# Query rows in overlapping groups of four, one buffer for a batch's rows, loads held back, in a fused attention and gated convolution

## The chip, the cores and the metric

The kernel runs on one core of one Trainium2 chip. The metric is the device time of one execution in microseconds (us); of several executions the median is taken. The core has five engines that run their own instruction streams: TensorE (PE), VectorE (DVE), the scalar engine (ACT), GpSimd (POOL) and SyncE (SP). SP issues the DMAs of this kernel's main part; they move data between HBM and SBUF, or inside SBUF.

## The reference

Agent attention, B = 4, N = 12800, C = 128, 49 agents, followed by a gated block with a causal convolution of five taps along the sequence:

```python
def sm(a, b):
    s = scale * (a @ b.transpose(0, 2, 1))
    s = s - s.max(-1, keepdims=True)
    e = np.exp(s)
    return e / (e.sum(-1, keepdims=True) + 1e-09)
a2k = sm(agents, k)
agent_v = a2k @ v
q2a = sm(q, agents)
x = q2a @ agent_v
...
for k in range(K):
    gate_pre += conv_w[k][None, None, :] * xp[:, k:k + S, :]
gate = 1.0 / (1.0 + np.exp(-gate_pre))
val = x @ w_val
return (gate * val @ w_out).astype(np.float32)
```

## The kernel before

A batch's 12800 positions are cut into 10 units of 1280, two units make a segment (20 in all), and 25 chunks of 512 positions a batch (the last one of all is halved) are what TensorE works on behind the softmax.

**Per batch.** Key scores are made (L376), their maximum is taken, they are exponentiated, and the agents' values are summed up (L480). Then the batch's weights are folded: since x is q2a times 49 rows, the value weights and the five convolution taps are multiplied with these 49 rows beforehand (gw at L541, wst), so that the chunks work on the rows of q2a and x is never formed. Weights and rows are float16, each split into a high part (hi) and the rest (lo), and hi x hi, hi x lo and lo x hi are summed.

**Per unit (queries, transposes).** Scores (L376), transposed on VectorE (sT), less their maximum (L750 on POOL, written to a ring `qw`), exp on ACT, sum, reciprocal and product on VectorE (L772). The float16 rows `pt` have 128 columns per block of 128 positions: lo in 0:49 (L794 on POOL, `w - hi`), hi in 49:98 (cast L779 on ACT), and 30 columns that repeat two of three hi columns (L784 on POOL). A transpose turns `pt` into 128 rows of 1280 positions: on TensorE for the first four units (L849), by a DMA transpose for the other 36 (L835). The rows go into one of four buffers `x1_` (ring NX = 4), one per segment, with 16 columns ahead of each. Of these the last four (HALO) hold the end of the segment before: POOL copies them (L819), or clears them at a batch's start (L816), when the transposes of the segment before have landed.

**x2.** What 128 rows have no room for, hi x lo for some hi rows, goes through a second tile `x2`: 19 hi rows, each five times, shifted by 0 to 4 positions, are copied from `x1_` by two DMAs inside SBUF (L884): 15 rows that stand three partitions apart (75 rows of x2) and four adjacent ones (20 rows). 95 of 128 partitions are in use.

**Per chunk.** The gate is five matmuls on x1, one per tap (L922), and one on x2 with 95 rows (L926); tanh on ACT (L935). The value is one matmul on x1 (L949) and one on x2 (L953). h is made on VectorE (L962), hh is its float16 part (ACT, L968), hl the rest (POOL, L973), and three matmuls with the output weights follow (L992, L993, L994). ACT scales the result (L1006), and a DMA on SP stores it (L1021).

**What sets the order.** TensorE's order is one long string written by hand (`order`). For the other engines, `Plan.order` places each step (with a cost written beside it) by list scheduling in a simulated time, and the program is then issued in the order of the steps' start times. SP's queue, in order, takes the loads (L369, 11 buffers `ld`), the transposes (L835), the x2 copies (L884) and the stores. A load is a step as soon as its buffer is free: the planner places it as early as the queue allows. `Plan.order` ends with

```python
self.start = start
return sorted(range(n), key=lambda i: (start[i], i))
```

Of the kernel before, what the change touches and what calls it, by code (L numbers as in the profile page):

```python
# [32 lines left out]
THREES = 15  # L33
NDUP = 2 * THREES
X2R = 19
X2CUTS = ((0, THREES, 3, 0.5), (THREES, X2R, 1, 0.3))

# [4 lines left out]
NX = 4  # L42
# [18 lines left out]
LAND = 1.4  # L61

# [5 lines left out]
class Plan:  # L68
# [25 lines left out]
    def order(self):  # L94
# [22 lines left out]
        at = [0.0] * n  # L117
# [56 lines left out]


@with_exitstack
def tile_agent_attention_gated_conv(
# [39 lines left out]
    qw = ring(NPT, [P, NBLK, A], F32, "qw")  # L217
# [3 lines left out]
    x1s = ring(NX, [P, PAD + SEG], F16, "x1_")  # L221
# [39 lines left out]
    tiny = const.tile([P, NBLK], F32, name="tiny")  # L261
    nc.scalar.dma_start(out=ag_sb, in_=agT)
# [6 lines left out]
    nc.vector.memset(x1s[0][:, 0:PAD], 0.0)  # L269
    for t in wst_sb:  # L270
        nc.gpsimd.memset(t[:, TAPS + 1 :, :], 0.0)
# [82 lines left out]
    def load(kind, b, u):  # L354
# [12 lines left out]
        for d, f, keys in parts:  # L367
            add(
                "dma", 0.4, lambda d=d, f=f: nc.sync.dma_start(out=d, in_=f), (), keys,  # L369
                1.57 / len(parts),  # L370
            )
# [132 lines left out]
    avT = const.tile([P, A], F32, name="avT")  # L504
    mx = const.tile([P, 2], F32, name="mx")
    gw = const.tile([P, TAPS, A], F32, name="gw")
    gs = const.tile([P, TAPS, A], F32, name="gs")
# [5 lines left out]
    def fold_weights(b):  # L513
# [19 lines left out]
        def normalise():  # L533
            dve.tensor_scalar_add(den, pt[:, 0:A], 1e-9)
            dve.reciprocal(out=den, in_=den)
            dve.tensor_tensor(out=avT, in0=pt[:, AP_ : AP_ + A], in1=den, op=ALU.mult)
# [5 lines left out]
                out=gw, in0=avT.unsqueeze(1).to_broadcast([P, TAPS, A]),  # L542
                in1=conv_sb.unsqueeze(2).to_broadcast([P, TAPS, A]), op=ALU.mult,
# [4 lines left out]
        def gate_scale():  # L548
# [16 lines left out]
                out=pv[:, 0:A], lhsT=wval_sb, rhs=avT, start=True, stop=True  # L565
# [4 lines left out]
        x2g = wst[:, TAPS + 1, 0 : TAPS * X2R].rearrange("p (r k) -> p k r", k=TAPS)  # L570
        x2v = wst[:, TAPS + 2, 0 : TAPS * X2R].rearrange("p (r k) -> p k r", k=TAPS)
        ghi = wst[:, 0:TAPS, 0:A]
        vhi = wst[:, TAPS, 0:A]

        def threes(x):

            if len(x.shape) == 2:
                return x[:, 0 : 3 * THREES].rearrange("p (i r) -> p i r", r=3)
            return x[:, :, 0 : 3 * THREES].rearrange("p k (i r) -> p k i r", r=3)

        def rest(out, full, s, hi):
            dve.scalar_tensor_tensor(
                out=out, in0=full, scalar=rs[:, s : s + 1], in1=hi,
                op0=ALU.mult, op1=ALU.subtract,
            )

        def val_weights():
# [9 lines left out]
            dve.tensor_scalar_mul(vhi, pv[:, 0:A], rs[:, 1:2])  # L597
            pv3, hi3 = threes(pv[:, 0:A]), threes(vhi)
            rest(
                wst[:, TAPS, 2 * A :].rearrange("p (i r) -> p i r", r=2),  # L600
                pv3[:, :, 0:2], 1, hi3[:, :, 0:2],
            )
            rest(x2v[:, HALO, 0:THREES], pv3[:, :, 2], 1, hi3[:, :, 2])
            rest(x2v[:, HALO, THREES:], pv[:, 3 * THREES : A], 1, vhi[:, 3 * THREES :])

        def gate_weights():
            dve.tensor_scalar_mul(ghi, gw, rs[:, 0:1])
# [6 lines left out]
        def gate_rest_pool():  # L614
            def less(out, full, hi):
                nc.gpsimd.tensor_tensor(out=out, in0=full, in1=hi, op=ALU.subtract)

            gs3, hi3 = threes(gs), threes(ghi)
            twos = wst[:, 0:TAPS, 2 * A :].rearrange("p k (i r) -> p k i r", r=2)
            for r in range(2):  # L620
                less(twos[:, :, :, r], gs3[:, :, :, r], hi3[:, :, :, r])
            less(x2g[:, :, 0:THREES], gs3[:, :, :, 2], hi3[:, :, :, 2])
            less(x2g[:, :, THREES:], gs[:, :, 3 * THREES :], ghi[:, :, 3 * THREES :])

        def gate_rest():
            gw3, hi3 = threes(gw), threes(ghi)
            twos = wst[:, 0:TAPS, 2 * A :].rearrange("p k (i r) -> p k i r", r=2)
            for r in range(2):
                rest(twos[:, :, :, r], gw3[:, :, :, r], 0, hi3[:, :, :, r])
            rest(x2g[:, :, 0:THREES], gw3[:, :, :, 2], 0, hi3[:, :, :, 2])  # L630
            rest(x2g[:, :, THREES:], gw[:, :, 3 * THREES :], 0, ghi[:, :, 3 * THREES :])
# [3 lines left out]
        if b == 0:  # L635
            add("pool", 0.4, gate_scaled, ["gw", "rsg"], ["gs"])
            add("act", 0.4, lambda: nc.scalar.copy(out=ghi, in_=gs), ["gs"], [(*w_, "g")])
            add("pool", 1.0, gate_rest_pool, ["gs", (*w_, "g")], [(*w_, "r")])
        else:
# [4 lines left out]
            lambda: nc.scalar.copy(out=wst[:, 0:TAPS, A : 2 * A], in_=ghi),  # L644
# [3 lines left out]
            "act", 0.22, lambda: nc.scalar.copy(out=wst[:, TAPS, A : 2 * A], in_=vhi),  # L648
# [84 lines left out]
    def queries(b, u):  # L733
# [4 lines left out]
        sT, d, e, w, r, sm = sts[x], qw[g % NPT], qw[g % NPT], qw[g % NPT], qr[x], qsm[x]  # L738
# [23 lines left out]
        def sums():  # L762
# [14 lines left out]
        p_ = ("pt", g % NPT)  # L777
        add(
            "act", 0.58, lambda: nc.scalar.copy(out=pt[:, :, A : 2 * A], in_=w),  # L779
# [3 lines left out]
            "pool", 0.44,  # L783
            lambda: nc.gpsimd.tensor_scalar(  # L784
                out=pt[:, :, 2 * A :].rearrange("p n (i r) -> p n i r", r=2),
                in0=w[:, :, 0 : 3 * THREES].rearrange("p n (i r) -> p n i r", r=3)[:, :, :, 0:2],
                scalar1=1.0, scalar2=0.0,
                op0=ALU.mult, op1=ALU.add,
# [3 lines left out]
        add(  # L792
            "pool", 1.09,
            lambda: nc.gpsimd.tensor_tensor(  # L794
                out=pt[:, :, 0:A], in0=w, in1=pt[:, :, A : 2 * A], op=ALU.subtract
            ),
            [("qw", g % NPT), (*p_, 0)], [(*p_, 1)],
        )
# [3 lines left out]

    def unit_rows(g):
        o = PAD + g % 2 * UNIT
        return x1s[g // 2 % NX][:, o : o + UNIT]

    def row_keys(s, halves):


        i = s % NX  # L810
        return [(x, i, h) for h in halves for x in ("x1", "x1b")] + [("x1h", i)] * (0 in halves)

    def halo(s):
        to = x1s[s % NX][:, PAD - HALO : PAD]
        if s * 2 % NU == 0:
            fn = lambda: nc.gpsimd.memset(to, 0.0)  # L816
            read = []
        else:
            fn = lambda: nc.gpsimd.tensor_copy(  # L819
                out=to, in_=x1s[(s - 1) % NX][:, PAD + SEG - HALO : PAD + SEG]  # L820
            )
            read = [(x, (s - 1) % NX, 1) for x in ("x1", "x1b")]

        read.append(("x2", (s - 1) % 3, UNIT, 0))
        add("pool", 0.1, fn, read, [("x1h", s % NX)])
# [40 lines left out]
    def shifts(b, u):  # L866
# [7 lines left out]
        x2, x1 = x2s[s % 3], x1s[s % NX]  # L874
        o = (g + 1 - n) % 2 * UNIT
        src = row_keys(s, range(0, g % 2 + 1))
        c = PAD - HALO + o
        for r0, r1, every, us in X2CUTS:
            first = A + (2 if every == 3 else 3 * THREES)
            rows = x1[first : first + 1 + (r1 - r0 - 1) * every : every, c : c + 1]  # L880
# [4 lines left out]
                    out=x2[r0 * TAPS : r1 * TAPS, o : o + n * UNIT],  # L885
# [255 lines left out]
    for i in plan.order():  # L1141
        plan.steps[i][2]()
# [44 lines left out]
```

## Time and profile before

Three executions took 425.65, 425.89 and 426.75 us, the median is 425.89.

| | value |
|---|---|
| median of the runs | 425.89 us |
| span of the profiled execution | 423.6 us |
| instructions in it | 10042 |
| DMA traffic | 127.62 MB, mean 301 GB/s |
| HBM read, written | 79.25 MB, 26.21 MB |

The profile is one execution, taken by the hardware profiler. Its span begins and ends with the first and last recorded work; what lies around it makes the 2.3 us to the median. Busy time is given per engine, and in rows of groups as `line engine operation out<-in, shape, count | busy us, mean ns of one | idle time just before, and what ended it`. In rows of waits the three numbers are us in total, times, and the longest. `PEclk` is the clock granted to TensorE in tenths. In rows of a timeline the start and the duration in us come first, and a bracket holds the idle time ahead and its releaser.

### The profile page before, as it was taken

To read this page: it belongs to the slowest core of one execution; us is meant where nothing else is said; L and a number is where in the kernel's file an instruction comes from. 1 tells how busy PE (TensorE), PEld (TensorE's weight loads), DVE (VectorE), ACT (ScalarE), POOL (GpSimd) and SP (SyncE) were. 2 spreads that over 40 slices of the span, in tenths; PEclk is the share of its full clock that TensorE was granted. 3 is DMA by queue.
4 is the path that set the end of the run, shared out by engine and by line. 5 is a ranking of instruction groups with operands and counts; after the bars stand their busy time and mean duration, and the time that the engine had idled before them with its cause. 6 is when DMAs were issued, how large, how long until landed. Compare 5 with 4: busy or idle time off the path is not lost.

```text
span 423.6 us, 10042 instructions
## 1 busy us (share of the span) xinstructions
PE 403.9 (95%) x3907; PEld 197.0 (47%) x3907; DVE 293.3 (69%) x562; ACT 301.5 (71%) x521; POOL 228.2 (54%) x263
## 2 busy tenths in 40 slices
PE   4979999999999999999999899999999989999995
PEld 1358434346555443446555343335555534344443
DVE  3757899867875978667795575767765678676231
ACT  1564568779966777678876486778876567788776
POOL 1002557654657565554566355574366277877553
PEclk9969999999999999999999899999999999999998
DMA  8999999999999999999999999999999977755733
GB/s 320 420 417 411 370 367 353 301 295 310 412 293 283 346 317 362 304 278 356 351 379 324 271 299 370 314 332 302 296 393 322 239 196 161 199 163 176 205 121 124
DMA packets 75129, 127.62 MB, mean 301 GB/s; under 512 B 50466, under 2 KB 50850, under 8 KB 75084
## 3 DMA queue, kind: packets, MB, share of 16 engines
q1 hardware_dynamic: 74940, 126.87, 96.9%
q8 instruction: 30, 0.49, 0.5%
q10 hardware_dynamic: 144, 0.13, 0.2%
q14 instruction: 15, 0.12, 0.1%
HBM read 79.25 MB, written 26.21 MB: 249 GB/s over the span
## 4 chain that ended last, share of the span: by engine, by line
PE 78%; DMA 9%; DVE 8%; ACT 1%; POOL 1%; issue 1%; SPq 0%; POOLq 0%; DVEq 0%; ACTq 0%
PE gate L922 23%; PE sc L376 17%; PE av L480 10%; PE val L949 5%; PE out L992 5%; PE val L953 5%; PE gate L926 5%; PE out L993 4%; DMA ld<-kT 4%; PE out L994 4%; DMA x<-pt 3%; DMA x<-x 2%; DVE h L962 1%; DVE qw L772 1%; DVE qsm L763 1%
## 5 line engine op out<-in xcount | busy, mean ns | idle before, releaser
L973 POOL TENSOR_TENSOR hl<-h,hh 128x512 f16<-128x512 f32 (+1 forms) x101 | 116.9, 1158 | 96.1 <-ACT hh L968 96.0
L922 PE MATMUL gate<-x,stat 128*128 128x512 f16 (+1 forms) x500 | 125.2, 380 | 0.2 <-ACT th L935 0.2
L962 DVE SCALAR_TENSOR_TENSOR h<-th,val 128x512 f32<-128x512 f32 x100 | 67.8, 678 | 66.8 <-PE out L993 26.2
L376 PE MATMUL sc<-ld,ag_sb 128*32 128x320 f32 x1280 | 101.5, 447 | 7.6 <-DMA ld<-kT 7.0
L935 ACT ACTIVATE th<-gate,unscale 128x512 f32<-128x512 f32 x100 | 68.3, 683 | 33.3 <-PE gate L926 31.7
L1006 ACT ACTIVATE ob<-out,oscale 128x512 f32<-128x512 f32 x98 | 67.3, 687 | 21.3 <-PE out L994 20.1
L922 PEld LDWEIGHTS <-stat 128*128 128x128 f16 x505 | 46.3, 97 | 63.7 <-issue 14.8
L968 ACT CAST hh<-h 128x512 f16<-128x512 f32 (+1 forms) x101 | 61.5, 609 | 17.2 <-DVE h L962 16.4
L750 POOL TENSOR_TENSOR qw<-sT,qmx 128x490 f32<-128x490 f32 x40 | 41.4, 1035 | 47.6 <-DVE qmx L745 47.5
L376 PEld LDWEIGHTS sc<-ld,ag_sb 128*32 128x32 f32 x1280 | 36.7, 111 | 59.4 <-issue 25.7
L480 PE MATMUL av<-ld,eT 128*32 128x129 f32 (+1 forms) x1400 | 50.7, 279 | 1.0 <-DVE eT L386 1.0
L480 PEld LDWEIGHTS av<-ld,eT 128*32 128x32 f32 (+1 forms) x1400 | 47.1, 117 | 7.5 <-issue 2.5
L794 POOL TENSOR_TENSOR pt<-qw,pt 128x490 f16<-128x490 f32 x40 | 44.8, 1120 | 3.1 <-ACT pt L779 2.9
L471 ACT ACTIVATE e<-ks,kbias 128x320 f32<-128x320 f32 x80 | 39.3, 554 | 5.4 <-DVE eT L386 3.3
L386 DVE STREAM_TRANSPOSE sT<-sc 128x640 f32<-128x640 f32 x40 | 33.6, 839 | 13.4 <-PE sc L376 12.7
L402 ACT COPY ks<-sc 128x640 f32<-128x640 f32 x40 | 27.7, 691 | 21.2 <-PE sc L376 19.1
L386 DVE STREAM_TRANSPOSE eT<-e 128x640 f32<-128x640 f32 x40 | 33.5, 842 | 9.8 <-ACT e L471 5.2
L926 PE MATMUL gate<-x,stat 95*128 95x512 f16 x100 | 38.3, 383 | 1.5 <-DMA x<-x 1.5
L949 PE MATMUL val<-x,stat 128*128 128x512 f16 x100 | 38.2, 382 | 0.8 <-DVE h L962 0.6
L953 PE MATMUL val<-x,stat 95*128 95x512 f16 x100 | 38.1, 381 | 0.0
L994 PE MATMUL out<-hl,wo 128*128 128x512 f16 x98 | 37.0, 378 | 1.1 <-POOL hl L973 1.1
L992 PE MATMUL out<-hh,wo 128*128 128x512 f16 x98 | 37.3, 381 | 0.1
(130 smaller groups left out, 389.4 us busy)
## 6 DMA issues: line engine op xcount, KB each, us to landing
ld<-kT SPq DMA_DIRECT2D x40, 640.0 KB
ld<-qT SPq DMA_DIRECT2D x40, 640.0 KB
ld<-vP SPq DMA_DIRECT2D x39, 645.0 KB
outT<-ob SPq DMA_DIRECT2D x48, 512.0 KB
x<-x SPq DMA_DIRECT2D x18, 375.0 KB
x<-x SPq DMA_DIRECT2D x18, 100.0 KB
outT<-ob SPq DMA_DIRECT2D x3, 256.0 KB
x<-x SPq DMA_DIRECT2D x4, 187.5 KB
```

The source lines that it names most:

```text
L376: nc.tensor.matmul(out=out[g * BLK : (g + 1) * BLK, j, 0:GT], lhsT=ag_sb[:, b, j * BLK : (j + 1) * BLK], rhs=src[:, g * GT : (g + 1) * GT] ...
L386: nc.vector.transpose(out=out.rearrange("p n (j i) -> p j n i", j=2), in_=in_.rearrange("p j (n i) -> p j n i", i=BLK),)
L480: nc.tensor.matmul(out=av[o + j : o + j + cols, 0 : C + 1], lhsT=et[:, n, j : j + cols], rhs=vt[:, n, :], start=(u == 0 and n < 2), stop=( ...
L922: nc.tensor.matmul(out=pg, lhsT=stat[:, k, :], rhs=x1[:, c : c + w], start=(k == 0), stop=False,)
L926: nc.tensor.matmul(out=pg, lhsT=stat[0 : TAPS * X2R, TAPS + 1, :], rhs=x2[0 : TAPS * X2R, o2 : o2 + w], start=False, stop=True,)
L935: lambda: nc.scalar.activation(out=th, in_=pg, func=AF.Tanh, scale=unscale[:, 0:1]),
L949: nc.tensor.matmul(out=pv, lhsT=stat[:, TAPS, :], rhs=x1s[(b * NCH + n0 // CH) // 5 % NX][:, PAD + o2 : PAD + o2 + w], start=True, stop=False,
L953: nc.tensor.matmul(out=pv, lhsT=stat[0 : TAPS * X2R, TAPS + 2, :], rhs=x2[0 : TAPS * X2R, o2 : o2 + w], start=False, stop=True,)
L962: lambda: nc.vector.scalar_tensor_tensor(out=h, in0=th, scalar=1.0, in1=pv, op0=ALU.add, op1=ALU.mult),
L968: "act", 0.16 + 0.42 * scale, lambda: nc.scalar.copy(out=hh, in_=h),
L973: lambda: nc.gpsimd.tensor_tensor(out=hl, in0=h, in1=hh, op=ALU.subtract),
L1006: lambda: nc.scalar.activation(out=ob[:, o : o + w], in_=po, func=AF.Copy, scale=oscale),
```

## The change

**Rows.** Each block's 128 columns are laid out anew: hi in rows 32 to 99 as 17 groups of four that overlap by one (each group of four begins with the last row of the group before it, so 49 values fill 68 rows), 11 repeated hi rows in 21:32, lo in 0:21 and 98:128 in two pieces. `qw` has 52 columns, the 49 values at 1:50, so that one ACT instruction writes the groups (680 elements instead of 490), POOL repeats 110 elements instead of 300, and the lo part takes two POOL instructions (210 and 300 elements).

**x2.** 22 rows instead of 19, taken from rows four partitions apart: 16 rows (80 partitions) and 6 rows (30 partitions), at partitions 16 to 125 of x2, whose other partitions are cleared once. The matmuls on x2 use all 128 partitions, in weights and rows.

**Fold.** The weights follow the same layout: two ACT copies instead of one for gate and for value, four VectorE (for the first batch's gate POOL) subtractions instead of three; `gs` borrows a store buffer.

**x1.** One buffer with five segments behind each other (a batch) and one stretch of 16 columns ahead of it. The end of a segment thereby stands in front of the next: POOL's copies and clears of four columns are gone, and the gate's matmuls of a segment read the last four columns of the one before.

**Loads.** A first run of the planner gives each step's start. A load is then held until 14 us (`AHEAD`) ahead of the earliest planned start of the steps that read it, and the planner runs again.

```diff
-THREES = 15
-NDUP = 2 * THREES
-X2R = 19
-X2CUTS = ((0, THREES, 3, 0.5), (THREES, X2R, 1, 0.3))
+AW = 52
+HI = 32
+FOURS = 17
+LOWS = ((HI + 4 * FOURS - 2, 0, 10), (0, 10, FOURS - 10))
+TWICE = 11
+AGAIN = HI - TWICE
+X2R = 22
+X2O = 16
+X2CUTS = ((0, 16, HI + 2, 0.5), (16, X2R, HI + 1 + 4 * TWICE, 0.2))
+def fours(x):
+    return x[:, :, HI : HI + 4 * FOURS].rearrange("p n (i r) -> p n i r", r=4)
+def threes(x, first, n, width):
+    ap = [tuple(d) for d in x.ap]
+    return bass.AP(x.tensor, x.offset + first, ap[:2] + [(3, n), (1, width)])
...
-NX = 4
+NX = 5
...
+AHEAD = 14.0
...
-        at = [0.0] * n
+        at = list(held or [0.0] * n)
...
+    def late_loads(self):
+        self.order()
+        held = [0.0] * len(self.steps)
+        for i, s in enumerate(self.steps):
+            for j in s[3]:
+                if self.steps[j][5] == "ld":
+                    t = self.start[i] - AHEAD
+                    held[j] = min(held[j], t) if held[j] else t
+        return self.order(held)
...
-    x1s = ring(NX, [P, PAD + SEG], F16, "x1_")
+    x1 = const.tile([P, PAD + NX * SEG], F16, name="x1")
...
     for t in wst_sb:
-        nc.gpsimd.memset(t[:, TAPS + 1 :, :], 0.0)
+        nc.gpsimd.memset(t, 0.0)
+    for t in x2s + qw:
+        nc.gpsimd.memset(t, 0.0)
...
+        def rests(full, hi, out, x2_, less):
+            n = X2R - 16
+            less(out[:, :, HI + 4 : HI + 4 * FOURS : 4], full[:, :, 2:A:3], hi[:, :, 0:16, 3])
+            less(out[:, :, AGAIN:HI], full[:, :, 0 : 3 * TWICE : 3], hi[:, :, 0:TWICE, 1])
+            less(x2_[:, :, 0:16], full[:, :, 1:A:3], hi[:, :, 0:16, 2])
+            less(x2_[:, :, 16:], full[:, :, 3 * TWICE : A : 3], hi[:, :, TWICE : TWICE + n, 1])
+        def lows(out, hi):
+            for to, i0, n in LOWS[::-1]:
+                nc.scalar.copy(
+                    out=out[:, :, to : to + 3 * n].rearrange("p k (i r) -> p k i r", r=3),
+                    in_=hi[:, :, i0 : i0 + n, 1:4],
+                )
...
-            "act", 0.58, lambda: nc.scalar.copy(out=pt[:, :, A : 2 * A], in_=w),
+            "act", 0.75, lambda: nc.scalar.copy(out=hi, in_=threes(wide, 0, FOURS, 4)),
...
+        def lower():
+            for to, i0, n in LOWS[::-1]:
+                nc.gpsimd.tensor_tensor(
+                    out=pt[:, :, to : to + 3 * n].rearrange("p n (i r) -> p n i r", r=3),
+                    in0=threes(wide, 1 + 3 * i0, n, 3), in1=hi[:, :, i0 : i0 + n, 1:4], op=ALU.subtract,
+                )
...
-            fn = lambda: nc.gpsimd.tensor_copy(
-                out=to, in_=x1s[(s - 1) % NX][:, PAD + SEG - HALO : PAD + SEG]
-            )
...
-            first = A + (2 if every == 3 else 3 * THREES)
-            rows = x1[first : first + 1 + (r1 - r0 - 1) * every : every, c : c + 1]
+            rows = x1[first : first + 1 + (r1 - r0 - 1) * 4 : 4, c : c + 1]
...
-                out=pg, lhsT=stat[0 : TAPS * X2R, TAPS + 1, :],
-                rhs=x2[0 : TAPS * X2R, o2 : o2 + w], start=False, stop=True,
+                out=pg, lhsT=stat[:, TAPS + 1, :], rhs=x2[:, o2 : o2 + w],
+                start=False, stop=True,
...
-    for i in plan.order():
+    for i in plan.late_loads():
         plan.steps[i][2]()
```

**Where it moves instructions.** TensorE's order stays the same. On SP, the place of segment 9 (counted from 0), whose copies go into the first x2 buffer (the number ahead is the row in SP's program, `ld` with its number the load buffer, qT, kT and vP what is loaded; in brackets stand the semaphores a row waits for, DMAHW0 to DMAHW7 being those that DMAs set when they have landed, given out in turn). Before:

```order
142 L369 DMA ld8_69<-kT 128x1280 [waits DMAHW6_49,PE_49]
143 L1021 DMA outT<-ob2_122 128x1024 [waits DMAHW7_49,Activation_49]
144 L369 DMA ld9_70<-kT 128x1280 [waits DMAHW0_49,PE_49]
145 L835 DMA_TRANSPOSE x1_1_102<-pt2_99 128x10x128 [waits DMAHW1_49,Pool_49]
146 L369 DMA ld10_71<-kT 128x1280 [waits DMAHW2_49,PE_49]
147 L835 DMA_TRANSPOSE x1_1_102<-pt3_100 128x10x128 [waits DMAHW3_49,Activation_49,Pool_49]
148 L1021 DMA outT<-ob3_123 128x1024 [waits DMAHW4_49,Activation_49]
149 L369 DMA ld0_61<-kT 128x1280 [waits DMAHW5_49,PE_49]
150 L369 DMA ld1_62<-qT 128x1280 [waits DMAHW6_49,PE_49]
151 L884 DMA x20_105<-x1_1_102 75x1x2560 [waits DMAHW7_49,DMAHW3_49,DMAHW1_49]
152 L884 DMA x20_105<-x1_1_102 20x1x2560 [waits DMAHW0_49]
153 L835 DMA_TRANSPOSE x1_2_103<-pt0_97 128x10x128 [waits Activation_49,Pool_49]
```

And with the change, at the same segment:

```order
138 L863 DMA_TRANSPOSE x1_101<-pt2_99 128x10x128 [waits DMAHW2_49,Activation_49,Pool_49]
139 L1047 DMA outT<-ob2_119 128x1024 [waits DMAHW3_49,Activation_49]
140 L863 DMA_TRANSPOSE x1_101<-pt3_100 128x10x128 [waits DMAHW4_49,Activation_49,Pool_49]
141 L404 DMA ld4_65<-qT 128x1280 [waits DMAHW5_49,PE_49]
142 L404 DMA ld5_66<-vP 128x1290 [waits DMAHW6_49,PE_49]
143 L911 DMA x20_102<-x1_101 80x1x2560 [waits DMAHW7_49,DMAHW4_49,DMAHW2_49]
144 L404 DMA ld6_67<-vP 128x1290 [waits DMAHW0_49,PE_49]
145 L911 DMA x20_102<-x1_101 30x1x2560 [waits DMAHW1_49]
146 L1047 DMA outT<-ob3_120 128x1024 [waits Activation_49]
147 L863 DMA_TRANSPOSE x1_101<-pt0_97 128x10x128 [waits DMAHW3_49,DMAHW1_49,DMAHW7_49,Activation_49,Pool_49]
148 L863 DMA_TRANSPOSE x1_101<-pt1_98 128x10x128 [waits Activation_49,Pool_49]
149 L404 DMA ld7_68<-qT 128x1280 [waits DMAHW5_49,PE_49]
```

The last load ahead of the copies was the one into buffer 1 (a round later); now it is the one into buffer 5. So the seven loads into buffers 6 to 10, 0 and 1 moved behind the first copy, and one of them stands between the two. The first transpose of the next segment (x1_2 from pt0 before, x1 from pt0 now) waited for engines only; it now also waits for three DMAs, among them the two copies, which read the same tile x1.

On POOL, the place of the fourth batch's fold (gw), where hl is the low part of h of a chunk and the row of L819 copies the four columns. Before:

```order
203 L784 TENSOR_SCALAR pt0_97<-qw0_89 128x10x30
204 L794 TENSOR_TENSOR pt0_97<-qw0_89,pt0_97 128x10x49
205 L819 COPY x1_0_101<-x1_3_104 128x4
206 L973 TENSOR_TENSOR hl0_117<-h0_111,hh0_114 128x512
207 L973 TENSOR_TENSOR hl1_118<-h1_112,hh1_115 128x512
208 L541 TENSOR_TENSOR gw_167<-avT_165,moe_sb_161 128x245
```

And with the change:

```order
230 L820 TENSOR_SCALAR pt0_97<-qw0_89 128x10x11
231 L829 TENSOR_TENSOR pt0_97<-qw0_89,pt0_97 128x10x21
232 L829 TENSOR_TENSOR pt0_97<-qw0_89,pt0_97 128x10x30
233 L999 TENSOR_TENSOR hl1_115<-h1_109,hh1_112 128x512
234 L575 TENSOR_TENSOR gw_172<-avT_144,moe_sb_167 128x255
```

The copy is gone from between the unit's rows and the low parts, the low rows take two instructions, and one of the two low parts now stands ahead of the rows.

More of the change, by code (lines that the diff above doesn't have):

```diff
@@ L92, in add, with order @@
         self.urge.append(urge)
-    def order(self):
+    def order(self, held=None):
         n = len(self.steps)
@@ L643, in fold_weights @@
             "act", 0.4,
-            lambda: nc.scalar.copy(out=wst[:, 0:TAPS, A : 2 * A], in_=ghi),
+            lambda: lows(wg, ghi),
             [(*w_, "g")], [(*w_, "d")],
```

143 lines of the change are left out of this document (58 added, 85 removed).

## The prediction

> **What bounds the kernel now.** I read the busy line and the slices of the page first, then the chain, then the waits of TensorE, and at last the stretches around the three waits that are left in mid-run.
>
> ```profile
> PE 403.9 (95%) x3907; PEld 197.0 (47%) x3907; DVE 293.3 (69%) x562; ACT 301.5 (71%) x521; POOL 228.2 (54%) x263
> ...
> PE   4979999999999999999999899999999989999995
> ...
> PEclk9969999999999999999999899999999999999998
> DMA  8999999999999999999999999999999977755733
> ...
> PE 78%; DMA 9%; DVE 8%; ACT 1%; POOL 1%; issue 1%; SPq 0%; POOLq 0%; DVEq 0%; ACTq 0%
> ```
>
> TensorE (PE) is busy 95% of the span of 423.6 us and is 78% of the chain that ended last, so the kernel is bound by it: 423.6 - 403.9 = 19.7 us are idle, and only two things shorten the run, less time per matmul or fewer of these idle microseconds. Two other marks matter. The DMA slices stand at 9 until four fifths of the span, so transfers queue for most of the run. The clock slices are at 9 except the third, the 23rd and the last, which show a lower clock. The idle time, by what ended it:
>
> ```profile
> PE sc L376 <- DMA ld<-kT: 7.0, 4, 6.1
> PE gate L926 <- DMA x<-x: 1.5, 1, 1.5
> ...
> PE out L994 <- POOL hl L973: 1.1, 1, 1.1
> ...
> PE val L949 <- DVE h L962: 0.6, 1, 0.6
> ```
>
> The first row is the wait for the first loads, which nothing in the change touches. The other three are waits in mid-run, and the change reaches all of them: the first is for the copies that fill x2 (the rows of a chunk's second matmul), the second for the low halves of h, made on GpSimd (POOL), and the third is an after-effect of the second, as will be seen.
>
> **The change part by part: the matmuls on x2.** They now use 128 rows where they had 95.
>
> ```profile
> L922 PE MATMUL gate<-x,stat 128*128 128x512 f16 x495 | 124.5, 381 | 0.2 <-ACT th L935 0.2
> ...
> L926 PE MATMUL gate<-x,stat 95*128 95x512 f16 x99 | 38.0, 384 | 1.5 <-DMA x<-x 1.5
> L949 PE MATMUL val<-x,stat 128*128 128x512 f16 x99 | 37.9, 383 | 0.8 <-DVE h L962 0.6 <-DVE wo L728 0.2
> L953 PE MATMUL val<-x,stat 95*128 95x512 f16 x99 | 37.9, 382 | 0.0
> L992 PE MATMUL out<-hh,wo 128*128 128x512 f16 x98 | 37.3, 381 | 0.1
> ...
> L993 PE MATMUL out<-hh,wo 128*128 128x512 f16 x98 | 37.0, 377 | 0.0
> ```
>
> A full-height matmul behind a full-height one (L993) takes 377 ns; the 95-row ones take 384 and 382, and so do the ones that directly follow a 95-row one in the order (L949 383, L992 381). Over L993 that is 7 + 6 + 5 + 4 = 22 ns in a chunk, and 99 chunks make 2.2 us. I read this as the price of a change of height in the row of matmuls. Two things make it less than sure: the durations overlap from one matmul to the next, so a delay may be counted twice, and the five gate matmuls of full height (L922) have a mean of 381 without any change of height inside their row. The term lies between 0 and -2.2, and I take -1.6, nearer to what the last five rows show.
>
> The Trainium skill, "TensorE: Matmul & The Clock Gate", section "🎯 Why this matters for your kernels", says of small matmuls: "K=32 single mm = same time as K=128". By that rule height is free, in both directions, and this term would be 0; the rows of L926 and L993 differ by 7 ns, so the trace speaks a little against it, with the reservation that position rather than height may be the cause.
>
> **The wait for x2 at 234 us.** This is the dearest of the three. On SP's queue, in the chain of waits, on TensorE and by stretches (PE busy, its weight loads, DVE, ACT, POOL, then granted clock, DMA share, GB/s) it reads:
>
> ```profile
> 212.77 7.23 SPq L835 DMA_TRANSPOSE x<-pt  x1
> ...
> 230.04 5.71 SPq L835 DMA_TRANSPOSE x<-pt  x2
> ```
> ```profile
> 220.73 7.50 DMA x<-pt
> ...
> 228.28 7.34 DMA x<-x
> ```
> ```profile
> 235.67 0.39 PE L926 MATMUL gate<-x,stat 95*128 95x512 f16 x1 [1.50 <-DMA x<-x]
> ```
> ```profile
> 234.00:236.00 2.00, 0.51 (x3) 0.21 (x3) 1.05 (x3) 0.32 (x1) 0.10 (x1) 1.00 0.66 137
> 236.00:238.00 2.00, 1.99 (x10) 1.01 (x8) 1.04 (x3) 1.03 (x2) 0.00 (x0) 0.75 1.21 360
> 238.00:240.00 2.00, 2.00 (x6) 0.73 (x5) 1.03 (x5) 0.62 (x2) 1.65 (x3) 0.50 0.99 275
> 240.00:242.00 2.00, 2.00 (x18) 1.04 (x20) 1.28 (x5) 1.19 (x3) 0.19 (x2) 0.90 0.97 297
> ```
>
> The first transpose of the segment is issued at 212.77 and holds SP's queue for 7.23 us; the second goes at 220.73 and lands 7.50 us later; only then are the x2 copies issued, at 228.28, and they land after 7.34 us. Together 212.77 to 235.62 is 22.9 us. TensorE stands still for 1.50 us, and right behind it the granted clock is low: 0.75, 0.50 and 0.90 over three stretches of 2 us, so 2 x (0.25 + 0.50 + 0.10) = 1.7 us of full-speed work are lost. The wait costs 1.5 + 1.7 = 3.2 us in all.
>
> The change holds a load back until 14 us, by the planner's clock, before its use. At this place seven loads that were queued ahead of the x2 copies come behind them, or between their two halves, so the DMA engines have less in hand when transposes and copies arrive; 7.23 us on SP and 7.3 us of landing are long against the 1.37 us that the same transpose takes there late in the run (below), where the DMA slices show 7 and less. It needs 1.5 us out of 22.9 us to clear the wait, a fourteenth. Against it: the x2 copies carry 110 rows instead of 95, 16% more, which at 7.34 us is 1.2 us if all of it scales. I take the wait as gone, with its slow clock: -3.2; the bounds are 0 and -3.2.
>
> The Trainium skill, on the same page and in the same section, gives a limit for what lowers the clock: "No PE-idle gaps >~3µs between matmul bursts". By that, 1.5 us would not, and this term would be 1.5 alone. Here the low clock stands directly behind the 1.50 us wait, and nowhere else after the start, so the measurement decides.
>
> **The halo copies.** With x1 as one long buffer, POOL no longer copies a segment's last four columns ahead of the next (L819, 16 copies).
>
> ```profile
> 338.78 0.19 POOL L819 COPY x<-x 128x4 f16<-128x4 f16 x1 [5.99 <-DMA x<-pt]
> 338.93 2.27 POOL L973 TENSOR_TENSOR hl<-h,hh 128x512 f16<-128x512 f32 x2
> 341.15 0.61 POOL L541 TENSOR_TENSOR gw<-avT,moe_sb 128x245 f32<-128x245 f32 x1
> ```
> ```profile
> POOL x L819 <- DMA x<-pt: 16.4, 5, 6.0
> ```
>
> POOL stood for 5.99 us at such a copy until a transpose had landed, with two low halves (hl) queued behind it. The matmul on the first of them waited 1.11 us, and the fold of the next weights (L541) came late too, at 341.15, then its work on VectorE and with it h, for which TensorE waited 0.58 us. Without the copies nothing on POOL waits for a DMA at this place. So -1.1 - 0.6 = -1.7, bounds 0 (another wait of POOL or VectorE in its place) and -1.7. POOL's other four waits at L819 (16.4 - 6.0 = 10.4 us) held no matmul and are worth nothing.
>
> **What the new layout costs on the other engines.**
>
> ```profile
> L973 POOL TENSOR_TENSOR hl<-h,hh 128x512 f16<-128x512 f32 x99 | 115.5, 1168 | 94.8 <-ACT hh L968 94.7
> ...
> L1006 ACT ACTIVATE ob<-out,oscale 128x512 f32<-128x512 f32 x98 | 67.3, 687 | 21.3 <-PE out L994 20.1 <-DMA x<-x 0.4 <-DMA outT<-ob 0.3
> ...
> L794 POOL TENSOR_TENSOR pt<-qw,pt 128x490 f16<-128x490 f32 x40 | 44.8, 1120 | 3.1 <-ACT pt L779 2.9
> ...
> L779 ACT CAST pt<-qw 128x490 f16<-128x490 f32 x40 | 23.9, 600 | 10.7 <-DVE qw L772 10.7
> ...
> L784 POOL TENSOR_SCALAR pt<-qw 128x300 f16<-128x300 f32 x40 | 18.2, 457 | 20.6 <-DVE qw L772 20.6
> ...
> L819 POOL COPY x<-x 128x4 f16<-128x4 f16 x16 | 3.0, 187 | 16.9 <-DMA x<-pt 16.4 <-issue 0.5
> ...
> L973 POOL TENSOR_TENSOR hl<-h,hh 128x256 f16<-128x256 f32 x2 | 1.3, 671 | 1.3 <-ACT hh L968 1.3
> ...
> L1006 ACT ACTIVATE ob<-sc,oscale 128x256 f32<-128x256 f32 x2 | 0.9, 475 | 0.6 <-PE sc L994 0.6
> ...
> L271 POOL MEMSET wst<- 128x256 f16 x2 | 0.6, 312 | 0.0
> ...
> L816 POOL MEMSET x<- 128x4 f16 x3 | 0.3, 102 | 0.0
> ```
>
> Scalar engine (ACT): 256 more elements cost 687 - 475 = 212 ns, 0.83 ns each. The cast of a unit (L779) writes 680 elements instead of 490: 190 x 0.83 = 158 ns, times 40 is 6.3 us, and ACT goes from 301.5 to 308, 73% of the span. POOL: hl shows (1168 - 671) / 256 = 1.94 ns an element and so 1168 - 512 x 1.94 = 175 ns for an instruction by itself. The low part (L794) covers 510 elements in two instructions instead of 490 in one: +0.2 us a unit; the copied rows (L784) fall from 300 elements to 110: 190 x 0.94 ns = 0.18 us less, by the slope of (457 - 175) / 300; the halos take 16 x 0.187 = 3.0 us with them. POOL's sum stays where it is, at 54%. None of this touches TensorE in mid-run: a unit's rows are wanted several chunks after they are made, and what ends the idle time of ACT and POOL is mostly TensorE's or VectorE's work. If that cover were gone, it would be 0.16 + 0.2 us a unit, 40 units, 14 us, which only an unbroken chain through both could bring.
>
> The memsets at the start, with (312 - 102) / 252 = 0.83 ns an element: two weight tiles of 1024 elements, three x2 of 2560 and four row buffers of 520, 11,800 elements or 9.8 us. Their cover:
>
> ```profile
> POOL qw L750 <- DVE qmx L745: 47.5, 15, 32.9
> ```
>
> POOL has nothing to do for 32.9 us ahead of its first query work. At the start of the run the chain from the first query rows to the first gate is in the open: the cast (+0.16), the second instruction (+0.18) and, at the fold, a second ACT copy for its fixed part, 687 - 512 x 0.83 = 262 ns. VectorE's work for the first query unit, however, comes earlier in its order. Bounds +1 and -0.5; I take +0.4.
>
> **New waits.** All transposes and x2 copies now work on one buffer, and the first transpose of a segment carries waits for the landing of the copies that read the segment before. SP is in order: behind such a transpose wait loads and stores. No row of the trace shows it; the nearest is the 7.34 us that a landing takes. I take +1.0 for small waits that follow (a third of a wait like the one at 234), with bounds 0 and +3.2, one whole such wait. Loads landed well ahead of use in the trace: among the waits of TensorE only those at the start are for ld.
>
> **The sum.** -1.6 - 3.2 - 1.7 + 0.4 + 1.0 = -5.1 us. The profiled execution has a span of 423.6 us; the median of the runs, 425.89, stands 2.3 above it, which I carry over: 425.9 - 5.1 = **420.8 us**. A measurement of this kernel can tell from no change what differs by over about 0.3%, 1.3 us: below 424.6 is faster, above 427.2 slower.
>
> **The rivals.**
>
> Slower: SP becomes the bound. A segment's own path in the backlog, transposes and x2 copies one after the other, took 22.9 us above; 20 segments share 423.6 us, 21.2 each. In the kernel before the next segment's transposes start at 230.04, long before the copies land at 235.62; now they may not. If the landings stay as long as that, each segment is 22.9 - 21.2 = 1.7 us late against TensorE, and the loads behind, issued only 14 us ahead, use up their margin: two more waits of the 3.2 us kind beside the one that stays give 425.9 - 1.6 - 1.7 + 0.4 + 6.4 = 429.4. It decides from the point at which the path of a segment exceeds 21.2 us. Against it: less queued ahead shortens just these landings, and transposes whose queue is empty hold SP for less:
>
> ```profile
> 372.59 1.37 SPq L835 DMA_TRANSPOSE x<-pt  x1
> ```
>
> Chance 0.19.
>
> The change doesn't do what it says: the DMA engines are as full as before, since the same loads follow a little later, and the wait at 234 stays. Then -1.6 - 1.7 + 0.4 + 1.0 = -1.9, 424.0. For it speaks the row of nines; against it the stretch from 234 to 236, in which TensorE waited while the DMA engines had a share of 0.66 and moved 137 GB/s, against 360 in the stretch behind. Chance 0.14.
>
> One new wait takes the place of the old one and another comes: 425.9 - 1.6 - 1.7 + 0.4 + 3.2 = 426.2, no change. Chance 0.13.
>
> Height is free: the waits go, and the 95-row matmuls were slow by their position, which stays: 420.8 + 1.6 = 422.4. Chance 0.12. (The rule of the Trainium skill on height, cited above, gives this case.)
>
> The low clock behind 236 is not tied to the wait and comes anyway, say from the thin work around it: 420.8 + 1.7 = 422.5. The rows, in which it stands directly behind the wait, give that 0.05. (The rule of the Trainium skill on gaps, cited above, gives this case.)
>
> **How the numbers follow.** The forecast itself has 0.37. Faster by over 0.3%: 0.37 + 0.14 + 0.12 + 0.05 = 0.68; within 0.3%: 0.13; slower by over 0.3%: 0.19. The low end takes every term at its best except the start: 425.9 - 2.2 - 3.2 - 1.7 = 418.8, less 0.5 for the start and some 1 us of the short waits not counted above, 417.3. The high end has to reach into the slower rival; with 428.0 about 0.15 lies above and 0.04 below 417.3.
>
> **What would show it.** Right: no PE wait for x<-x behind the start and a clock slice of 9 at 234; no wait of L994 for POOL near 340; the matmuls on x2 at 377 to 380 ns; ACT near 308 us, POOL near 228. Wrong: PE waits for ld in mid-run, long DMA_TRANSPOSE rows or gaps on SP behind x2 copies, or 383 ns on 128 rows.

## The result

| | before | with the change |
|---|---|---|
| median of the runs | 426.32 us (425.65 to 427.0, 4 runs) | 436.38 us (434.63 to 438.17, 4 runs) |
| span of the profiled execution | 423.6 us | 432.8 us |

The ratio is 1.0236, with a 95% interval of 1.0208 to 1.0264: slower by 10 us, where 420.8 us was forecast. The time lies above the range, and also above the rival that ended on the slower side, 429.4 us. Medians here are over all executions, while ratios leave out the few in a slower state, among them one of 827.74 us with loads 10 us ahead.

The profile after, first the busy line and the slices of the page:

```profile
PE 402.7 (93%) x3907; PEld 196.4 (45%) x3907; DVE 297.5 (69%) x567; ACT 307.4 (71%) x529; POOL 242.2 (56%) x291
...
PE   4878899999999998988999989999879999999996
...
PEclk9989999999999999998999999999999999999999
DMA  8999997999999989979999999999899779998743
```

TensorE is busy for about as long as before (402.7 us, 403.9 before), so the growth of the span by 9.2 us is idle time: 30.1 us now, 19.7 before. ACT is at 307.4 us, as worked out (308); POOL is at 242.2, which is 14 us more than the 228 expected. The PE row has six slices at 7 or 8 of ten between 160 and 325 us, where there was one before. The waits of TensorE name them:

```profile
PE sc L411 <- DMA ld<-kT: 10.4, 10, 6.0
PE sc L411 <- DMA ld<-qT: 3.7, 4, 1.9
PE av L515 <- DMA ld<-vP: 2.8, 4, 1.7
PE av L515 <- DVE qmx L780: 1.7, 1, 1.7
...
PE gate L952 <- DMA x<-x: 1.2, 1, 1.2
```

Before there were 7.0 us of waits for loads in four places, all at the start; now there are 16.9 us in 18 places, 9.0 us of them in ten places from 164 us on. The wait for x2 in mid-run and the one for hl are gone; the x2 wait that is left (1.2 us) is at 50 us. On SP's queue stands the row that was not there before:

```profile
SPq L863 <- DMA x<-x: 56.3, 17, 7.0
```

The DMA transposes (L863) waited 56.3 us in 17 places, up to 7.0 us each, for x2 copies to land. This is the new wait that the prediction named and priced at +1.0 us.

### The profile page after: what moved, and what is told of

Read it like the earlier page. It is cut to its first block, busy times and chain, and to the rows that moved or that the text cites. A ratio compares the mean times of both kernels' runs of the same rounds, so it can differ in the third digit from the quotient of the medians.

```text
span 432.8 us, 10077 instructions
## 1 busy us (share of the span) xinstructions
PE 402.7 (93%) x3907; PEld 196.4 (45%) x3907; DVE 297.5 (69%) x567; ACT 307.4 (71%) x529; POOL 242.2 (56%) x291
## 4 chain that ended last, share of the span: by engine, by line
PE 65%; DMA 22%; DVE 8%; issue 2%; ACT 1%; POOL 1%; SPq 0%; POOLq 0%; DVEq 0%
PE gate L948 20%; PE sc L411 13%; DMA ld<-vP 10%; PE av L515 8%; DMA ld<-kT 6%; PE val L975 4%; PE out L1018 4%; PE val L979 4%; PE out L1019 4%; PE gate L952 4%; PE out L1020 4%; DMA ld<-qT 3%; DMA x<-x 2%; DVE h L988 1%; DVE sT L421 1%
## 5 line engine op out<-in xcount | busy, mean ns | idle before, releaser
L829 POOL TENSOR_TENSOR pt<-qw,pt 128x210 f16<-128x210 f32 x80 | 55.1, 689 | 10.1 <-ACT pt L815 6.9
L515 PE MATMUL av<-ld,eT 128*32 128x129 f32 (+1 forms) x1400 | 52.0, 283 | 5.7 <-DMA ld<-vP 2.8
L952 PE MATMUL gate<-x,stat 128*128 128x512 f16 x100 | 37.8, 378 | 1.2 <-DMA x<-x 1.2
L975 PE MATMUL val<-x,stat 128*128 128x512 f16 x100 | 37.9, 379 | 0.9 <-DVE h L988 0.7
L815 ACT CAST pt<-qw 128x680 f16<-128x680 f32 x40 | 30.2, 755 | 11.0 <-DVE qw L807 10.8
L979 PE MATMUL val<-x,stat 128*128 128x512 f16 x100 | 37.8, 378 | 0.0
```

Source lines behind the costliest of these rows:

```text
L515: nc.tensor.matmul(out=av[o + j : o + j + cols, 0 : C + 1], lhsT=et[:, n, j : j + cols], rhs=vt[:, n, :], start=(u == 0 and n < 2), stop=( ...
L952: nc.tensor.matmul(out=pg, lhsT=stat[:, TAPS + 1, :], rhs=x2[:, o2 : o2 + w], start=False, stop=True,)
L975: nc.tensor.matmul(out=pv, lhsT=stat[:, TAPS, :], rhs=x1[:, o1 : o1 + w], start=True, stop=False,)
L979: nc.tensor.matmul(out=pv, lhsT=stat[:, TAPS + 2, :], rhs=x2[:, o2 : o2 + w], start=False, stop=True,)
```

## The experiments

Three things were changed at once: the row layout, the one buffer x1, and the held loads. Four runs take them apart, two isolate the wait, one tests the height of the matmuls on x2, and four vary how far ahead loads go.

**Loads not held.** The last line again takes the order without the hold:

```diff
-    for i in plan.late_loads():
+    for i in plan.order():
```

> The changed kernel with loads again placed as early as their buffers allow; new layout and one buffer x1 stay. Theory H (held loads are late: issue to first use fell from 19-33 us to 5-17 us, mid-run): the PE waits for ld vanish, 420 to 424 us. Theory T (the wait of each segment's first transpose for the landing of the x2 copies, 56 us of SP's time in 17 waits, makes everything on SP late): the waits on SP stay, 432 to 437 us. Theory HT (both are needed: 14 us would do on a queue that is not blocked): 421 to 426 us, with the SP waits still there.

446.46 us, ratio 1.050 (1.045 to 1.055): ten microseconds worse still than the changed kernel. The waits for loads in mid-run are gone, but so much more is lost at x2:

```profile
PE gate L952 <- DMA x<-x: 13.7, 5, 8.4
PE sc L411 <- DMA ld<-kT: 7.9, 4, 5.7
```
```profile
SPq L863 <- DMA x<-x: 62.2, 21, 8.1
```

So holding loads is not what makes the change slow (theory H falls); it softens it. The waits on SP stay, as theories T and HT had it, but the time is outside all three forecasts: none had seen that x2 copies come late when unheld loads and the wait meet.

**The hold alone, in the kernel before.** `late_loads` and the `"ld"` key of the loads are added to the kernel before; layout and x1 ring stay.

```diff
-                1.57 / len(parts),
+                1.57 / len(parts), key="ld",
...
-    for i in plan.order():
+    for i in plan.late_loads():
```

> The kernel before with nothing changed but the held loads (14 us); layout and the ring of x1 buffers as before. H: PE waits for ld in mid-run, 433 to 437 us. T: no such waits, 423 to 426 us, since x2 copies find less queued ahead. HT: few short waits for ld, 424 to 429 us.

428.07 us, ratio 1.0040 (1.0009 to 1.0070). A small loss, above what theory T allowed and within the range of HT: the wait at 234 us is gone (0.3 us of x2 waits are left), and 3.4 us of waits for vP came in its place.

```profile
PE av L493 <- DMA ld<-vP: 3.4, 3, 1.6
```

**A ring of x1 buffers with the change.** Layout and hold stay; x1 is again four buffers, with POOL's copies of four columns:

```diff
-    x1 = const.tile([P, PAD + NX * SEG], F16, name="x1")
+    x1s = ring(NX, [P, PAD + SEG], F16, "x1_")
...
+        if g % 2 and (g + 1) // 2 < B * NU // 2:
+            halo((g + 1) // 2)
```

> The changed kernel with a ring of four x1 buffers and POOL's copies of four columns as before; layout and held loads stay. H: 433 to 437 us, PE waits for ld as in the changed kernel. T: no SP wait of a transpose for x2 copies, 420 to 424 us. HT: 421 to 428 us.

422.36 us, ratio 0.9906 (0.9879 to 0.9933): 14.0 us faster than the changed kernel and 1% faster than the one before. SP has no wait of a transpose for x2 copies. Theory T and HT both allow it, H does not.

**The layout alone.** The same ring, and no hold.

```diff
-    for i in plan.late_loads():
+    for i in plan.order():
```

> The new row layout alone: ring of four x1 buffers with POOL's copies, loads as early as their buffers allow. All theories: no PE wait for ld in mid-run. If my terms of the layout hold (-1.6 us from full-height matmuls, +0.4 at the start), 424 to 426 us, with the x2 wait near 234 us and its low clock possibly there.

431.06 us, ratio 1.0122 (1.0087 to 1.0156), 5 us over the forecast of 424 to 426. The x2 wait did not come at 234 us but at 97 us (2.5 us), beside one of 1.5 us at 51 us. At 305 us there is an hl wait of 2.2 us behind one of POOL's copies, which had waited 6.93 us for a transpose, the same kind that the kernel before had at 340 us. Whether the x2 copies are late because they are 16% larger was not tested.

```profile
PE gate L963 <- DMA x<-x: 4.1, 2, 2.5
...
PE out L1031 <- POOL hl L1010: 2.2, 1, 2.2
```

**The wait alone.** A ring differs from one buffer by more than the wait. But the wait can be taken out by itself. The copies of a segment read up to the last column of their segment, and the transposes of the next one write from there on, so the columns do not overlap. The waits are put in when the program is built, by the ordering of accesses to one tile, and they depend on the length of the tile's rows: sixteen unused columns behind the fifth segment, and they are gone. (Why the length matters to it was not looked into.)

```diff
-    x1 = const.tile([P, PAD + NX * SEG], F16, name="x1")
+    x1 = const.tile([P, PAD + NX * SEG + 16], F16, name="x1")
```

Every engine's instructions and their order are the same as in the changed kernel; only waits differ. Row 147 of SP (the first transpose of segment 10), in the changed kernel and with the wider tile:

```
147 L863 DMA_TRANSPOSE x1_101<-pt0_97 128x10x128 [waits DMAHW3_49,DMAHW1_49,DMAHW7_49,Activation_49,Pool_49]
147 L863 DMA_TRANSPOSE x1_101<-pt0_97 128x10x128 [waits DMAHW3_49,Activation_49,Pool_49]
```

> The changed kernel with the tile x1 16 columns wider at its end, which nothing reads or writes. Every engine's instructions and their order are the same; only the waits of the transposes for the landing of the x2 copies of the segment before are gone. Theory T (this wait is the whole loss): 420 to 423 us, PE waits for ld in mid-run gone or under 0.5 us each. Theory B (one buffer costs by something else, a slower write or read in the long tile): 432 to 437 us.

422.43 us, ratio 0.9903 (0.9872 to 0.9934). This one edit takes 14 us off the changed kernel, so what theory T says of the changed kernel holds: the wait is the whole loss, and the rest of the change gains 1%. Theory B falls. The largest rows of TensorE's waits have none for x2 or hl, and those for kT are the start's (in mid-run one wait of 0.36 us for vP is left):

```profile
PE sc L411 <- DMA ld<-kT: 6.6, 4, 5.7
PE val L467 <- DVE m L460: 1.4, 1, 1.4
PE av L515 <- DVE eT L421: 1.0, 1, 1.0
PE sc L411 <- DVE sT L421: 0.8, 1, 0.8
PE val L975 <- DVE h L988: 0.7, 2, 0.5
PE gate L948 <- ACT th L961: 0.7, 2, 0.5
```

How a wait on SP becomes one on TensorE shows in the timeline of SP at one place, first of the changed kernel, then of the wider tile, the same instructions of both (start, duration, then what is issued):

```profile
160.97 1.21 SPq L404 DMA_DIRECT2D ld<-qT  x1
166.53 3.59 SPq L863 DMA_TRANSPOSE x<-pt  x1
...
185.33 1.77 SPq L911 DMA_DIRECT2D x<-x  x2
187.22 0.37 SPq L404 DMA_DIRECT2D ld<-qT  x1
```
```profile
160.76 0.42 SPq L404 DMA_DIRECT2D ld<-qT  x1
161.27 5.73 SPq L863 DMA_TRANSPOSE x<-pt  x1
...
178.95 1.44 SPq L911 DMA_DIRECT2D x<-x  x2
180.51 0.37 SPq L404 DMA_DIRECT2D ld<-qT  x1
```

Until the load at 161 us both are within 0.2 us. Then the transpose stands for 4.4 us in the changed kernel (162.18 to 166.53) and goes at once with the wider tile. The x2 copies and the load behind it, with nothing new of their own to wait for, are 6.4 and 6.7 us late (two more transposes stand between). The chain of waits and the timeline of TensorE in the changed kernel show where that load ends:

```profile
187.22 6.68 DMA ld<-qT
```
```profile
193.95 1.28 PE L411 MATMUL sc<-ld,ag_sb 128*32 128x320 f32 x16 [1.11 <-DMA ld<-qT]
196.95 0.87 PE L515 MATMUL av<-ld,eT 128*32 128x129 f32 x12 [1.71 <-DVE qmx L780]
```

The load lands after 6.68 us, at 193.90, and TensorE has waited 1.11 us for it, then 1.71 us for VectorE's work on these scores. Of the 14 us that a load is held ahead, by the planner's clock, 6.7 us on SP and 6.7 us of landing leave 0.6.

**The wider tile without the hold.** The sixteen columns, and the same line as for the layout alone.

> The same 16 columns, and loads as early as their buffers allow. If late x2 copies are what held loads cure: near the layout alone (431 us), less what POOL's copies of four columns cost there, so 427 to 431 us, with PE waits for x2. If holding does nothing once the wait is gone: 420 to 423 us.

427.68 us, ratio 1.0033 (0.9996 to 1.0070). With the wait gone, the hold is worth 427.68 - 422.43 = 5.2 us. Most of that are x2 copies that come late when loads go ahead of them, in four places:

```profile
PE gate L952 <- DMA x<-x: 4.3, 4, 1.7
```

Against the layout with the ring (431.06) this is 3.4 us less. The ring has POOL's copies but also one buffer fewer, and no run parts the two. With held loads the medians do not differ (422.36 and 422.43), though the profiled execution of the ring still shows a copy that cost time (under the halo copies below).

**126 rows.** The two matmuls on x2 are cut to 126 rows:

```diff
-                out=pg, lhsT=stat[:, TAPS + 1, :], rhs=x2[:, o2 : o2 + w],
+                out=pg, lhsT=stat[0:126, TAPS + 1, :], rhs=x2[0:126, o2 : o2 + w],
```

> The same 16 columns, with the matmuls on x2 cut from 128 rows to 126 (the two rows left out are zeros, so nothing of the computation is missing). If a change of height between matmuls is what made the rows of 384 and 382 ns, they come back and the time rises by 1 to 2 us; if 95 rows as such or the position did, the rows stay at 378 to 380 ns and the time is the same within 0.5 us.

422.92 us, ratio 0.9914 (0.9885 to 0.9943); the total does not tell it from 128 rows, where 1 to 2 us were expected of a change of height. The mean durations of the matmuls on x2 rise to 381 and 380 ns from 379, not to 384 and 382. What tells them apart are the starts of the same matmul (the last one of a chunk, on hl) before and behind the same twelve chunks, in which none of the three kernels waits. In order the kernel before, the wider tile (128 rows), the wider tile with 126 rows:

```profile
240.73 0.38 PE L994 MATMUL out<-hl,wo 128*128 128x512 f16 x1
...
288.32 0.38 PE L994 MATMUL out<-hl,wo 128*128 128x512 f16 x1
```
```profile
238.48 0.38 PE L1020 MATMUL out<-hl,wo 128*128 128x512 f16 x1
...
285.97 0.38 PE L1020 MATMUL out<-hl,wo 128*128 128x512 f16 x1
```
```profile
239.46 0.38 PE L1020 MATMUL out<-hl,wo 128*128 128x512 f16 x1
...
287.06 0.38 PE L1020 MATMUL out<-hl,wo 128*128 128x512 f16 x1
```

47.59, 47.49 and 47.60 us, at a granted clock of 1.00 in all three: 128 rows save 0.10 us in twelve chunks, 8 ns a chunk, and 126 rows save nothing. The same stretch takes 47.49 us in the ring with held loads and in the wider tile without the hold as well, so the difference is not chance. It is not the 95 rows as such that cost, and neither is it their position; whether it is the change of height in the row or any height under 128 was not told apart. It comes to 0.8 us in 100 chunks.

**How far ahead.** Loads 20, 16 and 10 us ahead with the wider tile, and 24 us ahead in the changed kernel as it is:

```diff
-AHEAD = 14.0
+AHEAD = 20.0
```

> The same 16 columns, loads held until 20 us ahead instead of 14. If 14 us leaves short waits for loads, up to 1 us faster than with 14; if the queue in front of the x2 copies is what counts, the same or up to 4 us slower. I expect within 1 us of the run with 14.

> x1 16 columns wider, loads held until 16 us ahead: between 14 us (422.4) and 20 us (424.3), so 421.5 to 424 us; a search for the better value rather than a test.

> x1 16 columns wider (no waits of transposes for x2 copies), loads held until 10 us ahead. With 14 us the loads land only 0 to 3 us before use from 245 us on; 4 us less should make PE wait for ld several times, 428 to 440 us. If loads have more room than this reading says: 421 to 425 us.

> The changed kernel as it is (x1 not widened, so the transposes wait for the x2 copies), loads held until 24 us ahead instead of 14. If its loss is only that blocked SP eats up the loads' 14 us: 422 to 427 us, no PE wait for ld. If the blocked queue costs either way, first the loads, then the x2 copies behind more loads: PE waits for x2 in their place, between the 436 us with 14 us and the 446 us without holding.

20 us: 424.32 us, ratio 0.9956 (0.9923 to 0.9988), 1.9 us above the run with 14 us where within 1 us was expected. 16 us: 426.34 us, ratio 0.9969 (0.9935 to 1.0003), outside what was expected, with runs from 421.55 to 427.49 us; the profiled execution was one of the short ones (span 420.4), so where the long ones lose is not shown. So the time does not follow the hold from 14 over 16 to 20 us in order. 10 us: 429.87 us, ratio 1.0070 (1.0043 to 1.0096); TensorE waits for kT ten times, 10.2 us in all (7.3 us in seven places at the start, 2.9 us in three later), and twice for vP, a loss of the kind expected at its lower edge. 24 us in the changed kernel: 433.32 us, ratio 1.0129 (1.0098 to 1.0159). There the loads come in time and the x2 copies do not, as the second expectation had it, though it ended just below the times named there:

```profile
PE sc L411 <- DMA ld<-kT: 8.0, 4, 5.9
PE gate L952 <- DMA x<-x: 7.2, 5, 2.8
```
```profile
SPq L863 <- DMA x<-x: 65.0, 21, 7.3
```

Side by side, medians in us (before: 426.3 to 426.8 in these sets):

| x1 | loads unheld | held, 14 us |
|---|---|---|
| old layout, ring | the kernel before | 428.07 |
| new layout, ring, POOL's copies | 431.06 | 422.36 |
| new layout, one buffer with the wait | 446.46 | 436.38 (the change) |
| new layout, one buffer, 16 columns wider | 427.68 | 422.43 |

The wait costs 18.8 us unheld and 14.0 us held. With held loads, the ring and the wider tile are both about 4 us faster than the kernel before, and 14 us faster than the changed kernel.

## Why the prediction was wrong

**The step that failed is "New waits", the term of +1.0 us with bounds 0 and +3.2.** The wait was named with its place, the queue behind it and the landing time of 7.34 us, but it was priced as one wait of TensorE. It recurs in nearly every segment: 17 waits, 56.3 us on SP, 3.3 us each. The wider tile, which has the same instructions without it, is 14.0 us faster, so +14.0 stands where +1.0 was put. The nearest row was right, and what was missing is the count: 18 segments with DMA transposes, each up to 7 us late on an in-order queue, against loads that the same change brought to within 14 us of their use. A product alone would have overshot, though. The waits of all transposes add up to 152.6 us in the changed kernel and to 120.2 us with the wider tile, where POOL's and ACT's work on the rows ends them instead; so 32.4 us of waiting are new on SP, and they cost the run 14.0 us. "Loads landed well ahead of use in the trace" was true of a trace in which loads were not held; that row could carry no bound for the new kernel.

**The slower rival** had the mechanism (SP in order, transposes behind landings, loads behind transposes), but it was built from the path of a segment, 22.9 us against 21.2, and from two extra waits for x2 of the 3.2 us kind. What happened does not need the path to exceed 21.2 us: it is the margin of single loads that is used up, at some ten places of 0.3 to 1.9 us.

**The wait for x2 at 234 us, -3.2.** Right in size. From the last matmul of the chunk before it to that of the chunk with it, before and with the wider tile:

```profile
232.71 0.38 PE L994 MATMUL out<-hl,wo 128*128 128x512 f16 x1
```
```profile
233.81 0.38 PE L1020 MATMUL out<-hl,wo 128*128 128x512 f16 x1
```

240.73 - 232.71 = 8.02 us against 238.48 - 233.81 = 4.67: 3.35 us less. That held loads are enough for it is shown by the kernel before with the hold alone: its x2 waits fell from 1.5 us to 0.3. That they were needed at this place is not: in the wider tile without the hold this wait is gone too, and four others stand elsewhere. (In the working, 1.5 us of 22.9 is a fifteenth, not a fourteenth; and the last clock slice, where TensorE has run out of work, is low as well.)

**The halo copies, -1.7.** Partly right. The 1.11 us for hl are gone. For h, TensorE still waits 0.48 us at that place with the wider tile, where it was 0.58, but not for the same reason: in the kernel before with the hold alone, where the copy ended earlier, no wait for h is left. VectorE's order shows another reason, before and with the wider tile:

```profile
345.56 0.64 DVE L962 SCALAR_TENSOR_TENSOR h<-th,val 128x512 f32<-128x512 f32 x1
346.12 0.66 DVE L772 TENSOR_TENSOR qw<-qw,qr 128x490 f32<-128x490 f32 x1
```
```profile
341.82 0.67 DVE L807 TENSOR_TENSOR qw<-qw,qr 128x490 f32<-128x490 f32 x1
342.40 0.68 DVE L988 SCALAR_TENSOR_TENSOR h<-th,val 128x512 f32<-128x512 f32 x1
```
```profile
343.13 0.38 PE L975 MATMUL val<-x,stat 128*128 128x512 f16 x1 [0.48 <-DVE h L988]
```

The product for the next query unit now stands ahead of h, and its 0.6 us are more than the wait (no run changed this order back). So -1.2 net. With the new layout two more such waits appear, which the prediction put at nothing ("None of this touches TensorE in mid-run"): 0.24 us for h at 146.65 and 0.48 us for tanh at 197.60. As to the copies with held loads: in the profiled execution of the ring, POOL stood 2.62 us at the copy of this place, and TensorE waited 1.03 us for tanh and 1.13 us for h behind it, 1.7 us more than with the wider tile. The medians do not show it.

**The start, +0.4.** Right in size. From the first matmul to the last one of the first chunk it takes 59.31 us before (6.10 to 65.41) and 59.66 with the wider tile (5.68 to 65.34).

**The matmuls on x2, -1.6.** There is a price, since 126 rows lose the gain; its size was 0.8 us. What was too large is the sum of four differences of mean durations (22 ns a chunk), where the starts give 8 ns; the prediction's own caution, that overlapped durations may count a delay twice, fits this. The Trainium skill, "TensorE: Matmul & The Clock Gate", section "🎯 Why this matters for your kernels", has a single matmul of 32 rows take the time of one with 128, which no run here contradicts; what these runs add is that a row of matmuls of 128 rows with two of 126 among them is 8 ns a chunk slower than one of 128 throughout. The measured 0.8 us lies midway between the rival's 0 and the forecast's 1.6.

**POOL's sum, "stays where it is".** Wrong by 14 us: 242.2 against 228.2. The low part was costed at +0.2 us a unit and took 2 x 0.689 us where it had taken 1.120, so +0.26. TensorE waits for it at one place, 0.62 us at 52 us with the wider tile (0.2 us before); otherwise it was hidden, as assumed.

```profile
L829 POOL TENSOR_TENSOR pt<-qw,pt 128x210 f16<-128x210 f32 x80 | 55.1, 689 | 10.1 <-ACT pt L815 6.9
```

That is (2 x 0.689 - 1.120) x 40 = 10.3 us of it (the row means pieces of 210 and of 300 elements). The memsets at the start, 9.8 us by the prediction's own estimate and 11.1 us in the profile, were left out of its sum. The copies (3.0 us) and the shorter repeated part (18.2 us before, 13.4 now, where 7 us less were expected) take some of both away again.

## What to carry to other kernels

When a change merges several buffers into one, list the waits that the merged tile gives to each queue and multiply them by how often they come; here a wait of a few microseconds on an in-order DMA queue delayed every load behind it, and with loads issued just in time TensorE paid for it. Waits that no overlap of data calls for could here be removed without touching an instruction: compare the waits of the two programs row by row, and try another row length of the tile. Where two edits act on the same queue, run them as a table of both; here the hold was worth +1.3, -8.7, -10.1 or -5.2 us, by what stood beside it.

## What had not been expected of the hardware

The wait of 1.50 us at 234 us in the kernel before was followed by 3.4 us of low clock, and the prediction took such a wait to cost 1.7 us more each time. That does not hold. In the changed kernel TensorE waited 1.90 us until 320.79, and the stretches around it (TensorE busy 0.90 and 1.21 us of 2.00) kept a clock of 1.00; the two waits at 194 and 197, 1.11 and 1.71 us with 1.3 us of work between them, were followed by a low one:

```profile
318.00:320.00 2.00, 0.90 (x5) 0.20 (x2) 0.69 (x1) 1.61 (x3) 1.96 (x2) 1.00 0.84 229
320.00:322.00 2.00, 1.21 (x16) 0.42 (x16) 0.00 (x0) 2.00 (x5) 1.40 (x2) 1.00 0.98 402
322.00:324.00 2.00, 1.72 (x46) 1.25 (x43) 1.04 (x2) 0.61 (x2) 1.12 (x2) 1.00 1.03 427
```
```profile
194.00:196.00 2.00, 1.23 (x16) 0.36 (x16) 1.72 (x3) 2.00 (x5) 1.27 (x2) 1.00 1.01 415
196.00:198.00 2.00, 1.05 (x21) 1.08 (x25) 1.57 (x3) 1.93 (x5) 1.98 (x2) 0.74 1.02 421
198.00:200.00 2.00, 2.00 (x47) 2.00 (x41) 0.55 (x1) 0.65 (x2) 0.00 (x0) 0.50 1.02 420
```

In the changed kernel with loads 24 us ahead even a wait of 2.83 us, until 340.19, was followed by a clock of 1.00. So the length of a single wait does not decide it; what does was not settled by these runs. The Trainium skill, "TensorE: Matmul & The Clock Gate", section "🔬 Part 1: The HAM clock gate (the "warmup" mystery)", says that the clock is set by activity in a window that runs freely, about 3.4 us long. That would fit two waits of 1.90 and 1.50 us with opposite outcomes, and the 3.4 us of low clock (1.7 us lost at half clock), but no run here varied where a wait falls.
